# The hand-over from attention to the MLP, written out by hand up to step 8

## The chip, the core and the metric

The kernel runs on one core of a Trainium2 chip. The metric is the device time of a run in microseconds (us). The kernel before takes 806.33 us, the median of three runs from 805.54 to 807.37. The profiled execution is one more run of the same program. The engines are named as in the profile: PE (TensorE, matrix products), PEld (its weight loads), DVE (VectorE), ACT (ScalarE), POOL (GpSimd) and SP (SyncE, which issues DMAs). Each works off its own queue in order; semaphores tie the queues together.

## The reference

Two parts follow each other. The first is attention over 2 batches, 8 heads, 768 positions and 64 dimensions, in which a query sees only keys of its own cluster (the cluster is the centroid with the largest dot product of normalized vectors). The second is two MLP layers on the 1536 x 512 result.

```python
mask = q_assign[:, :, :, None] == k_assign[:, :, None, :]
scores = np.where(mask, scale * np.matmul(q, k.transpose(0, 1, 3, 2)), -1000000000.0)
attn = np.exp(scores - np.max(scores, axis=-1, keepdims=True))
attn = attn / (np.sum(attn, axis=-1, keepdims=True) + 1e-09)
x = np.matmul(attn, v)              # -> (1536 tokens, 512)
h = x @ w_in                        # layer 1: 512 -> 2048
g = np.maximum(h, 0.0) + alpha * np.minimum(h, 0.0)
x = g @ w_out                       # 2048 -> 512
h = x @ w_in2                       # layer 2
g = np.maximum(h, 0.0) + np.log1p(np.exp(-np.abs(h)))
out = g @ w_out2
```

## The kernel before

Every matrix product of the MLP is made of three, since an operand is held as a high and a low part (xh and xl for the tokens, ih/il and oh/ol for the two weights, gh and gl for the activated values): high by high, high by low, low by high.

**Attention.** The heads are taken as 8 pairs, and each pair as 12 units of 128 queries, so there are NU = 96 units. A loop over ticks u (L812) issues for each tick the scores of unit u (tile s, two banks), the exponentials of unit u-1 on ACT (L614), the transposes pt of unit u-2 (L627) with their copies ph on ACT (L643) and low parts pl on DVE (L647), and an output group o of an earlier unit (L657). A finished output is drained: copied by ACT (tmp, L680) and added by DVE (xs, L682). Steps of other work are hung on a tick by the table `todo`, at an early (E) or late (L) place in it. The end of each pair is `finish` (L698): sums plus epsilon on POOL, reciprocals on DVE, a broadcast rx on ACT (L729), three transposes rp on PE (L739), the division on DVE (L745), each in two halves, then xh on ACT (L752) and xl on POOL (L757). The table FINISH gives the ticks, FINISH_LAST those of the last pair.

**Weights.** They arrive as 64-bit words. `to_float32` (L152) converts one 128x512 tensor in seven turns: a DMA raw; m on ACT (L164); r on ACT and a clamp of m on DVE (L167, L168); a shift of m on DVE (L171); r on DVE (L173); t on POOL (L178); the high part on ACT (L180) and the low part on POOL (L181). A block F has two tensors, and there are 32 blocks; five are held at a time.

**MLP.** The 96 steps (layer, token group g of 512, block f) each have 24 products: 12 first products into hp (`first`, L876), and, after `activate` (ACT, L888 and L889) and `complete` (DVE L909, ACT gh L916, DVE gl L917), 12 second products into four accumulators acc (`second`, L935). After the last block of a group `close` moves the accumulators to y (L947, ACT). Blocks come in sets of 2, 4, 4, 4, 2 in layer 1, so steps 0 to 5 use two weight blocks for three token groups.

**What sets the order.** Up to tick 96 the written order of the code is each engine's order (`manual_schedule`). From there on (L813) a scheduler with its own model of time orders the rest, and may place it among the last manual ticks. The MLP's code starts after the attention pools are closed: `first` is called two steps ahead of `second`, and a step's conversions are written out all at once (`conversions`). The MLP's hp and acc lie in pools of PSUM of their own, opened after the attention.

Of the kernel before, what the change touches and what calls it, by code (L numbers as in the profile page):

```python
# [9 lines left out]
F32 = mybir.dt.float32  # L10
# [40 lines left out]
FINISH_LAST = [1, 2, 2, 3, 6, 7, 8, 9, 9]  # L51

BLOCKS = ((2, 4, 4, 4, 2), (4, 4, 4, 4))
P = 128
# [4 lines left out]
def kernel(  # L59
# [134 lines left out]

    with ExitStack() as actx:
# [5 lines left out]
        ps_s = actx.enter_context(tc.tile_pool(name="ps_s", bufs=2, space=PSUM))  # L201
        ps_t = actx.enter_context(tc.tile_pool(name="ps_t", bufs=2, space=PSUM))
        ps_o = actx.enter_context(tc.tile_pool(name="ps_o", bufs=1, space=PSUM))
        ps_m = actx.enter_context(tc.tile_pool(name="ps_m", bufs=1, space=PSUM))
# [3 lines left out]
        def warm(n):  # L208

            wps = ps_t.tile([P, 512], F32, tag="t", name="wps")  # L210
            for _ in range(n):
                nc.tensor.transpose(wps[:, 0:P], ident, ident)
# [56 lines left out]
        warm(18)  # L269
# [428 lines left out]
        def finish(n):  # L698
# [6 lines left out]
            ks = FINISH_LAST if last else FINISH  # L705
# [27 lines left out]
            for t in range(2):  # L733

                @at_(u0 + ks[4 + t])
                def _(t=t):
                    rp_ = ps_m.tile([P, 512], F32, tag="m", name="rp_")
                    for j in range(3):
                        nc.tensor.transpose(  # L739
                            rp_[:, j * P : (j + 1) * P],  # L740
                            q["rx"][:, 3 * t + j].rearrange("p h d -> p (h d)"),
                            ident,
                        )
                    xs = xs_[n]
                    nc.vector.tensor_tensor(out=xs[:, halves[t]], in0=xs[:, halves[t]], in1=rp_[:, 0:HS], op=ALU.mult)  # L745
# [8 lines left out]
            @at_(u0 + ks[8])  # L754
            def _():
                xs = xs_.pop(n)
                nc.gpsimd.tensor_tensor(  # L757
                    out=xl[:, i, where], in0=xs, in1=xh.bitcast(F32)[:, i, where], op=ALU.subtract
                )
# [26 lines left out]
        started = {}  # L786
        stage = {}
# [6 lines left out]
        def temp0(which, dtype):  # L794
            return stage["cpool"].tile([P, DM], dtype, tag=which, name=which, bufs={"raw": 3, "m": 2, "t": 2}.get(which, 1))
# [6 lines left out]
        for F in range(4):  # L802
            todo[NU - 14 if F < 2 else NU - 12 + 6 * F, L].append(lambda F=F: begin(F))
            for j in range(2):
                start = NU - 12 + 3 * (2 * F + j)
                for n, wait in enumerate((0, 2, 3, 4, 5, 6, 8) if F < 2 else (0,)):
                    tick = NU - 14 if n == 0 and 2 * F + j < 3 else start + wait
                    todo[tick, L].append(lambda F=F, j=j: next(started[F][j]))

        LAG = 2 + QT  # L810
        u = 0
        while u < NU + LAG + 2 or todo:  # L812
            if u == NU:  # L813
                man.close()
# [24 lines left out]
        man.close()  # L839
# [4 lines left out]
    gp = ctx.enter_context(tc.tile_pool(name="gp", bufs=2, reuse_waits="tile"))  # L844
    sp = ctx.enter_context(tc.tile_pool(name="sp", bufs=1, reuse_waits="tile"))
    cp = ctx.enter_context(tc.tile_pool(name="cp", bufs=2, side="right", reuse_waits="tile"))
    ps_h = ctx.enter_context(tc.tile_pool(name="ps_h", bufs=4, space=PSUM, reuse_waits="tile"))
    ps_a = ctx.enter_context(tc.tile_pool(name="ps_a", bufs=1, space=PSUM, reuse_waits="tile"))

    steps, starts, ends = [], set(), set()  # L850
    for layer in range(2):
        f0 = 0
        for size in BLOCKS[layer]:
            starts.add((layer, f0))
            ends.add((layer, f0 + size - 1))
            steps += [(layer, g, f) for g in range(NG) for f in range(f0, f0 + size)]
            f0 += size
    NS = len(steps)
    hps = {}
    mids = {}  # L860
    acts = {}
    accs = {}
    sums_ = {}

    def first(k):
        if k >= NS:
            return
        layer, g, f = steps[k]
        ts = slice(g * G, (g + 1) * G)
        h_, l_ = weights[layer, f][0:2]  # L870
        hp = ps_h.tile([P, G], F32, tag="h", name="hp")
        n = 0
        for c in range(NC_):
            cs = slice(c * P, (c + 1) * P)
            for a_, b_ in ((h_, xh), (h_, xl), (l_, xh)):
                nc.tensor.matmul(hp, lhsT=a_[:, cs], rhs=b_[:, c, ts], start=n == 0, stop=n == 3 * NC_ - 1)  # L876
                n += 1
        hps[k] = hp

    def activate(k):  # L880
        if k >= NS:
            return
        layer, g, f = steps[k]
        hp = hps[k]
        if layer == 0:

            n = gp.tile([P, G], F32, tag="n", name="n")
            nc.scalar.activation(out=n, in_=hp, func=AF.Relu, scale=-1.0)  # L888
            nc.scalar.activation(out=hp, in_=hp, func=AF.Relu)  # L889
            mids[k] = n  # L890
        else:

            a = gp.tile([P, G], F32, tag="n", name="a")
            nc.vector.tensor_scalar(  # L894
                out=a.bitcast(U32), in0=hp.bitcast(U32), scalar1=0x80000000, scalar2=None, op0=ALU.bitwise_or
            )
            sp_ = gp.tile([P, G], F32, tag="sp", name="sp")
            nc.scalar.activation(out=sp_, in_=a, func=AF.Softplus)  # L898
            mids[k] = sp_

    def complete(k):

        if k >= NS:
            return
        layer, g, f = steps[k]
        b_ = mids.pop(k)
        hp = hps.pop(k)
        if layer == 0:
            nc.vector.scalar_tensor_tensor(  # L909
                out=hp, in0=b_, scalar=nalpha[:, f : f + 1], in1=hp, op0=ALU.mult, op1=ALU.add  # L910
            )
        else:
            nc.vector.scalar_tensor_tensor(out=hp, in0=hp, scalar=0.0, in1=b_, op0=ALU.max, op1=ALU.add)
        gh = gp.tile([P, G], F32R, tag="gh", name="gh")
        gl = gp.tile([P, G], F32R, tag="gl", name="gl")
        nc.scalar.copy(out=gh, in_=hp)  # L916
        nc.vector.tensor_tensor(out=gl, in0=hp, in1=gh.bitcast(F32), op=ALU.subtract)  # L917
        acts[k] = gh, gl

    def second(k):  # L920
        layer, g, f = steps[k]
        gh, gl = acts.pop(k)
        h_, l_ = weights[layer, f][2:4]
        opens, closes = (layer, f) in starts, (layer, f) in ends
        if opens:
            for c in range(4):
                accs[c] = ps_a.tile([P, 512], F32, tag=f"acc{c}", name=f"acc{c}")
        for c in range(4):
            cs = slice(c * P, (c + 1) * P)
            if layer == 0:  # L930
                prods = ((h_[:, cs], gh), (h_[:, cs], gl), (l_[:, cs], gh))
            else:
                prods = ((gh[:, cs], h_), (gh[:, cs], l_), (gl[:, cs], h_))
            for n, (a_, b_) in enumerate(prods):
                nc.tensor.matmul(  # L935
# [137 lines left out]
```

## Time and profile before

| | |
|---|---|
| median of three runs | 806.33 us (805.54 to 807.37) |
| span of the profiled execution | 804.5 us, 1.83 us below that median |
| PE busy | 780.4 us (97%), 4139 products and transposes |
| PEld busy | 666.7 us (83%) |
| DVE busy | 585.3 us (73%) |
| ACT busy | 496.0 us (62%) |
| POOL busy | 356.8 us (44%) |
| chain that ended last | PE 78%, DVE 11%, ACT 3%, POOL 3%, issue 3% |

The profile is of one execution, for which the results give no device time beside the span. A busy share is an average over two stages: the attention, up to about 260 us, and the MLP after it. Products overlap on PE, so the time from one start to the next tells more than the duration in a row. The granted clock is given as a share of full speed: 1.00 is 2.4 GHz, 0.50 is 1.2 GHz, and values between are stretches with both.

### The profile page before, as it was taken

The numbers are of one execution on the slowest core, as the hardware profiler recorded it, in microseconds if no ns is written. First come the engines' busy times: TensorE is split into PE (matmuls) and PEld (weight loads), VectorE is DVE, ScalarE is ACT, GpSimd is POOL, SyncE is SP. The second block draws the span as 40 slices with busy tenths as digits, with TensorE's granted clock in tenths as the row PEclk, the third lists the DMA queues.
The fourth block names the chain that finished last, engine by engine and source line by source line (L and its number), as shares of the span: only waits on it lengthen the run. The fifth ranks groups of instructions, "written<-read, shape, count | busy, mean of one in ns | idle before, by whom it ended". The sixth has DMA issues, their size and how long they took to land.

```text
span 804.5 us, 11964 instructions
## 1 busy us (share of the span) xinstructions
PE 780.4 (97%) x4139; PEld 666.7 (83%) x4139; DVE 585.3 (73%) x923; ACT 496.0 (62%) x1024; POOL 356.8 (44%) x380
## 2 busy tenths in 40 slices
PE   6899999999998979999999999999999999999998
PEld 6789999999997758888888888888888888888886
DVE  7689989989989977547646835978469569765444
ACT  5788999999999778346536535674366245343221
POOL 6567668778354775026115404585144036023000
PEclk9899999999999989999999999999999999999999
DMA  9666667655552343102302401312014012000002
GB/s 265 180 166 172 152 170 173 182 145 128 119 144 64 105 157 132 53 26 79 105 0 72 138 1 53 132 53 78 1 53 156 2 53 81 24 2 1 28 31 97
DMA packets 26955, 75.91 MB, mean 94 GB/s; under 512 B 4464, under 2 KB 7408, under 8 KB 26896
## 3 DMA queue, kind: packets, MB, share of 16 engines
q1 hardware_dynamic: 26896, 75.16, 32.3%
q8 instruction: 32, 0.52, 0.3%
q14 instruction: 27, 0.22, 0.1%
HBM read 49.36 MB, written 3.15 MB: 65 GB/s over the span
## 4 chain that ended last, share of the span: by engine, by line
PE 78%; DVE 11%; ACT 3%; POOL 3%; issue 3%; DMA 1%; SPq 0%; DVEq 0%; POOLq 0%; ACTq 0%
PE acc L935 29%; PE hp L876 27%; PE pt L627 6%; PE o L657 6%; PE s L599 3%; PE s L600 3%; DVE r L173 2%; DVE pl L647 2%; POOL t L178 1%; DVE nm L605 1%; PE dps L403 1%; DVE m L168 1%; DVE y L950 1%; DVE lo L388 1%; ACT e L614 1%
## 5 line engine op out<-in xcount | busy, mean ns | idle before, releaser
L876 PE MATMUL hp<-xh,ih 128*128 128x512 f32 x384 | 150.2, 392 | 1.3 <-ACT e L614 1.3
L876 PE MATMUL hp<-xl,ih 128*128 128x512 f32 x384 | 150.1, 391 | 0.0
L876 PE MATMUL hp<-xh,il 128*128 128x512 f32 x384 | 149.9, 391 | 0.0
L181 POOL TENSOR_TENSOR il<-t,ih 128x512 fp32r<-128x512 f32 x32 | 44.3, 1385 | 198.7 <-ACT ih L180 188.3
L917 DVE TENSOR_TENSOR gl<-hp,gh 128x512 fp32r<-128x512 f32 x96 | 65.9, 686 | 69.6 <-ACT gh L916 69.5
L916 ACT CAST gh<-hp 128x512 fp32r<-128x512 f32 x96 | 56.4, 587 | 88.8 <-PE acc L935 69.9
L605 DVE TENSOR_REDUCE nm<-s 128x1 f32<-128x768 f32 x96 | 90.9, 947 | 18.3 <-PE s L600 18.3
L647 DVE TENSOR_TENSOR pl<-pt,ph 128x384 fp32r<-128x384 f32 x192 | 97.3, 548 | 5.8 <-ACT ph L643 4.9
L178 POOL TENSOR_TENSOR t<-m,r 128x512 uint32<-128x512 uint32 x64 | 85.6, 1337 | 30.8 <-DVE r L173 16.3
L643 ACT CAST ph<-pt 128x384 fp32r<-128x384 f32 x192 | 84.0, 485 | 14.7 <-PE pt L627 14.1
L614 ACT ACTIVATE e<-s,nm 128x768 f32<-128x768 f32 x96 | 87.9, 916 | 3.0 <-DVE nm L605 2.4
L898 ACT ACTIVATE sp<-a 128x512 f32<-128x512 f32 x48 | 30.4, 632 | 92.5 <-DVE a L894 92.5
L627 PE MATMUL pt<-ident,e 128*128 128x128 f32 x576 | 83.2, 277 | 4.1 <-DVE pl L647 4.0
L876 PEld LDWEIGHTS hp<-xh,ih 128*128 128x128 f32 x384 | 72.4, 189 | 16.5 <-ACT e L614 1.6
L876 PEld LDWEIGHTS hp<-xh,il 128*128 128x128 f32 x384 | 72.5, 189 | 15.2
L876 PEld LDWEIGHTS hp<-xl,ih 128*128 128x128 f32 x384 | 72.4, 189 | 15.1
L627 PEld LDWEIGHTS pt<-ident,e 128*128 128x128 f32 x576 | 66.9, 141 | 16.4 <-DVE pl L647 13.0
L935 PE MATMUL acc<-gh,oh 128*128 128x512 f32 x192 | 72.6, 395 | 5.4 <-ACT gh L916 5.4
L935 PE MATMUL acc<-gl,oh 128*128 128x512 f32 x192 | 75.7, 394 | 0.2 <-DVE gl L917 0.2
L935 PE MATMUL acc<-gh,ol 128*128 128x512 f32 x192 | 75.2, 392 | 0.0
L935 PE MATMUL acc<-ol,gh 128*128 128x512 f32 x192 | 74.7, 389 | 0.0
L935 PE MATMUL acc<-oh,gh 128*128 128x512 f32 x192 | 74.7, 389 | 0.0
(171 smaller groups left out, 1671.8 us busy)
## 6 DMA issues: line engine op xcount, KB each, us to landing
raw<-in_w_in_dram SPq DMA_DIRECT2D x32, 512.0 KB, 3.3
raw<-in_w_out_dram SPq DMA_DIRECT2D x32, 512.0 KB, 3.3
tok<-in_qk_tok_dram SPq DMA_DIRECT2D x8, 768.0 KB, 6.1
ak<-hi SPq DMA_DIRECT2D x31, 192.0 KB, 3.0
dim<-in_qk_dim_dram SPq DMA_DIRECT2D x6, 768.0 KB, 5.4
aq<-hi SPq DMA_DIRECT2D x16, 192.0 KB, 3.6
aq<-lo SPq DMA_DIRECT2D x16, 192.0 KB, 4.1
rawv<-in_v_dram SPq DMA_DIRECT2D x8, 384.0 KB, 3.5
```

Of the source, the lines that this page charges most:

```text
L178: nc.gpsimd.tensor_tensor(out=t.bitcast(U32), in0=mu, in1=r, op=ALU.add)
L181: nc.gpsimd.tensor_tensor(out=low, in0=t, in1=high.bitcast(F32), op=ALU.subtract)
L605: nc.vector.tensor_reduce(out=nm, in_=st[u]["s"][:, :, 0:HS], axis=AX.XY, op=ALU.max, negate=True)
L614: nc.scalar.activation(out=e.rearrange("p (a j) c -> p a (j c)", a=2), in_=st[u]["s"][:, :, 0:HS], func=AF.Exp, bias=st[u]["nm"], scale=1. ...
L627: nc.tensor.transpose(pt[:, j * P : (j + 1) * P], st[u]["e"][:, 3 * a + j, :], ident)
L643: nc.scalar.copy(out=dh, in_=src)
L647: nc.vector.tensor_tensor(out=dl, in0=src, in1=dh.bitcast(F32), op=ALU.subtract)
L657: nc.tensor.matmul(acc[key][:, 0:QG], lhsT=vv[:, j, 2 * hh : 2 * hh + 2, :].rearrange("p a d -> p (a d)"), rhs=grp[key][part][:, j, :], st ...
L876: nc.tensor.matmul(hp, lhsT=a_[:, cs], rhs=b_[:, c, ts], start=n == 0, stop=n == 3 * NC_ - 1)
L916: nc.scalar.copy(out=gh, in_=hp)
L917: nc.vector.tensor_tensor(out=gl, in0=hp, in1=gh.bitcast(F32), op=ALU.subtract)
L935: nc.tensor.matmul(accs[c], lhsT=a_, rhs=b_, start=opens and n == 0, stop=closes and n == 2)
```

## The change

The four PSUM pools of the attention are opened outside it, and the score pool (two tiles of two banks) is closed at tick 96. Its space is opened at once as ps_h, four single banks for hp. The accumulators no longer have a pool of their own; they take the two transpose banks, the output bank and the spare bank of the attention. The functions of the MLP are moved ahead of the attention's loop, unchanged but for these places and for `work`, which gives step 0 its tiles from the attention's buffers. A table hangs step 0 on ticks 96 to 101, its first products in two pieces, and the written order goes on to step 8 (MANUAL): first products three steps ahead, conversions in single turns (`pump`), begun three turns apart, four turns in a step. From step 8 the scheduler orders as before. Besides: the last pair but one finishes in ticks 87 to 98 (FINISH_NEXT), the last pair's two transpose groups come ahead of its two divisions, and its xl is made in two halves by DVE and POOL; the conversion of blocks 2 and 3 begins some ticks later; the tiles of the activation have four buffers where they had two.

```diff
-FINISH_LAST = [1, 2, 2, 3, 6, 7, 8, 9, 9]
+FINISH_NEXT = [3, 4, 5, 6, 7, 8, 9, 10, 14]
+FINISH_LAST = [1, 2, 2, 3, 3, 3, 5, 5, 5]
+MANUAL = 8
...
+    def first(k, chunks=(0, 1, 2, 3)):
+        if k not in hps:
+            hps[k] = stage["ps_h"].tile([P, G], F32, tag="h", name="hp")
+        for c in chunks:
...
+        if opens:
+            for c in range(4):
+                pool, tag = ((ps_t, "t"), (ps_t, "t"), (ps_o, "o"), (ps_m, "m"))[c]
+                accs[c] = pool.tile([P, 512], F32, tag=tag, name=f"acc{c}")
...
+    def enqueue(F):
+        for gen in started.pop(F, None) or convert(F, stage["wpool"], temp):
+            if F >= 4:
+                next(gen)
+            queue.append((max(turn[0], queue[-1][0] + 3 if queue else 0), gen))
+    def pump(n=1):
+        for _ in range(n):
+            for begun, gen in queue:
+                if begun <= turn[0] < begun + 6:
+                    next(gen)
+            turn[0] += 1
...
-            ks = FINISH_LAST if last else FINISH
+            ks = FINISH_LAST if last else FINISH_NEXT if n == len(pairs) - 2 else FINISH
...
+                if last:
+                    at_(u0 + ks[4 + t])(lambda t=t: spread(t))
+                    at_(u0 + 4)(lambda t=t: divide(t))
...
+                    for eng, cut in zip((nc.vector, nc.gpsimd), halves):
+                        eng.tensor_tensor(
+                            out=xl[:, i, where][:, cut], in0=xs[:, cut],
...
-        for F in range(4):
-            todo[NU - 14 if F < 2 else NU - 12 + 6 * F, L].append(lambda F=F: begin(F))
+        for F, tick in ((2, NU + 1), (3, NU + 4)):
+            todo[tick, L].append(lambda F=F: begin(F))
...
+        def banks_pass():
+            scores_ctx.close()
+            stage["ps_h"] = ctx.enter_context(tc.tile_pool(name="ps_h", bufs=4, space=PSUM, reuse_waits="tile"))
+        todo[NU, E].insert(0, banks_pass)
+        for tick, phase, fn in (
+            (0, L, lambda: first(0, (0, 1))),
+            (2, E, lambda: first(0, (2, 3))),
+            (2, E, lambda: activate(0)),
+            (2, L, lambda: enqueue(2)),
+            (2, L, pump),
+            (3, L, lambda: complete(0)),
+            (3, L, pump),
+            (4, L, lambda: first(2, (0, 1, 2))),
+            (4, L, pump),
+            (5, L, lambda: second(0)),
+            (5, L, lambda: first(1)),
+            (5, L, pump),
+            (5, L, lambda: first(2, (3,))),
...
-            if u == NU:
-                man.close()
...
-    gp = ctx.enter_context(tc.tile_pool(name="gp", bufs=2, reuse_waits="tile"))
+    stage["gp"] = ctx.enter_context(tc.tile_pool(name="gp", bufs=4, reuse_waits="tile"))
...
-    ps_a = ctx.enter_context(tc.tile_pool(name="ps_a", bufs=1, space=PSUM, reuse_waits="tile"))
...
+    activate(1)
+    activate(2)
+    for F in (3, 4):
+        enqueue(F)
+    complete(1)
+    pump()
+    first(3)
+    activate(3)
+    complete(2)
+    pump()
+    for k in range(1, MANUAL):
+        second(k)
+        close(k)
+        pump()
+        for F in due.get(k, []):
+            enqueue(F)
+        complete(k + 2)
+        pump()
+        first(k + 3)
+        activate(k + 3)
+        pump(2)
+    pump(20)
+    man.close()
+    for k in range(MANUAL, NS):
...
-    for k in range(NS):
-        complete(k + 1)
-        if k < 2:
-            conversions(k)
-        first(k + 2)
-        activate(k + 2)
-        second(k)
-        close(k)
-        if k >= 2:
-            conversions(k)
```

What this does to the queues is seen in the order of the instructions. PE, from the last-but-one group of transposes to the first output group behind step 0's products, before (rp are the transposes for a division, hp the first products, o the output):

```order
L739 MATMUL rp__4314<-ident,rx 128x128 x3
L627 MATMUL pt<-ident,e 128x128 x6
L876 MATMUL hp<-xh,ih 128x512
...
L876 MATMUL hp<-xh,il 128x512
L657 MATMUL o<-ph,vv 128x256 x6
L657 MATMUL o<-pl,vv 128x256 x6
L627 MATMUL pt<-ident,e 128x128 x6
```

The same place now, as far as the transposes for the last division:

```order
L760 MATMUL pt<-ident,e 128x128 x6
L790 MATMUL o<-ph,vv 128x256 x6
L231 MATMUL hp<-xh,ih 128x512
...
L231 MATMUL hp<-xh,il 128x512
L760 MATMUL pt<-ident,e 128x128 x6
L790 MATMUL o<-pl,vv 128x256 x6
...
L790 MATMUL o<-ph,vv 128x256 x6
L790 MATMUL o<-pl,vv 128x256 x6
L874 MATMUL rp__4346<-ident,rx 128x128 x3
L874 MATMUL rp__4350<-ident,rx 128x128 x3
```

An output group has moved ahead of step 0's products; these stand in two pieces with a transpose group and an output group between them, and the last division's transposes follow directly. ACT, the instructions ahead of the activated value gh of step 2, before (y copies an accumulator, oh and ih are high parts of weights, m and r steps of a conversion):

```order
L947 COPY y<-acc_4477 128x512
L947 COPY y<-acc_4478 128x512
L180 CAST oh<-t 128x512
L947 COPY y<-acc_4479 128x512
L164 ACTIVATE m<-raw 128x512
L167 ACTIVATE r<-raw 128x512
L947 COPY y<-acc_4480 128x512
...
L888 ACTIVATE n<-hp 128x512
L889 ACTIVATE hp<-hp 128x512
...
L916 CAST gh<-hp 128x512
```

ACT now, from the products of step 0 to the drain of the last output (rx is the broadcast for the division, tmp the copy of an output):

```order
L813 COPY tmp<-o 64x256
L250 ACTIVATE n<-hp 128x512
L251 ACTIVATE hp<-hp 128x512
L862 COPY rx<-rs 128x384
L182 CAST ih<-t 128x512
L166 ACTIVATE m<-raw 128x512
L862 COPY rx<-rs 128x384
L278 CAST gh<-hp 128x512
L169 ACTIVATE r<-raw 128x512
L813 COPY tmp<-o 64x256
L902 CAST xh<-xs 128x384 x2
```

Step 0's activation stands between two drains, with single turns of conversions among the broadcasts; the copies of accumulators, which stood ahead of n, come behind three activations.

## Rows read from the trace of the kernel before

**Rows 1.** stretches: length, busy us (instructions) by engine, clock, DMA share, GB/s

```profile
248.93:258.74 9.81, 7.75 (x52) 6.33 (x52) 9.57 (x16) 8.88 (x21) 4.40 (x6) 1.00 0.35 115
258.74:263.92 5.18, 3.56 (x27) 2.87 (x25) 5.14 (x10) 5.13 (x13) 1.93 (x2) 1.00 0.03 6
263.92:268.37 4.45, 4.45 (x12) 3.49 (x13) 4.36 (x8) 3.68 (x8) 4.29 (x4) 0.62 0.29 113
...
291.68:297.21 5.53, 0.15 (x1) 0.00 (x1) 5.46 (x9) 5.53 (x12) 3.56 (x3) 0.79 0.53 176
297.21:302.37 5.16, 5.12 (x13) 3.60 (x13) 5.12 (x8) 5.16 (x11) 3.28 (x3) 0.56 0.37 133
302.37:800.64 498.27, 498.11 (x2197) 411.90 (x2195) 320.69 (x472) 233.06 (x414) 159.60 (x119) 1.00 0.17 57
```

**Rows 2.** waits of PE, 240 to 320: us in total, times, longest

```profile
PE acc L935 <- ACT gh L916: 5.4, 1, 5.4
```

**Rows 3.** timeline of PE: start, us, line, output<-inputs, [idle before <-releaser]

```profile
258.74 0.34 PE L599 MATMUL s<-ak,aq 128*128 128x384 f32 x1
...
260.15 0.94 PE L657 MATMUL o<-pl,vv 128*128 128x256 f32 x6
261.38 0.55 PE L739 MATMUL rp__4314<-ident,rx 128*128 128x128 f32 x3 [0.28 <-ACT rx L729]
261.76 0.82 PE L627 MATMUL pt<-ident,e 128*128 128x128 f32 x6
263.92 0.61 PE L876 MATMUL hp<-xh,ih 128*128 128x512 f32 x1 [1.34 <-ACT e L614]
...
297.21 2.08 PE L935 MATMUL acc<-gh,oh 128*128 128x512 f32 x4 [5.38 <-ACT gh L916]
```

**Rows 4.** timeline of ACT, at the last scores and before the wait

```profile
260.81 0.51 ACT L729 COPY rx<-rs 128x384 f32<-128x384 f32 x1
...
262.49 0.36 ACT L680 COPY tmp<-o 64x256 f32<-64x256 f32 x1
262.88 0.90 ACT L614 ACTIVATE e<-s,nm 128x768 f32<-128x768 f32 x1
...
265.11 0.68 ACT L167 ACTIVATE r<-raw 128x512 uint32<-128x512 uint32 x1
...
292.93 0.61 ACT L888 ACTIVATE n<-hp 128x512 f32<-128x512 f32 x1
...
296.56 0.60 ACT L916 CAST gh<-hp 128x512 fp32r<-128x512 f32 x1
```

**Rows 5.** timeline of DVE at the hand-over

```profile
251.07 0.41 DVE L171 TENSOR_SCALAR m<-m 128x512 uint32<-128x512 uint32 x1
...
262.54 0.51 DVE L745 TENSOR_TENSOR xs<-xs,rp__4314 128x384 f32<-128x384 f32 x1
...
263.96 0.42 DVE L682 TENSOR_TENSOR xs<-tmp,o 64x256 f32<-64x256 f32 x1
...
269.38 1.39 DVE L171 TENSOR_SCALAR m<-m 128x512 uint32<-128x512 uint32 x1
```

**Rows 6.** groups of instructions by line: busy us in total, mean ns

```profile
L178 POOL TENSOR_TENSOR t<-m,r 128x512 uint32<-128x512 uint32 x64 | 85.6, 1337 | 30.8 <-DVE r L173 16.3 <-DVE m L171 10.4 <-PE acc L935 1.0
...
L917 DVE TENSOR_TENSOR gl<-hp,gh 128x512 fp32r<-128x512 f32 x96 | 65.9, 686 | 69.6 <-ACT gh L916 69.5
L173 DVE SCALAR_TENSOR_TENSOR r<-raw,r 128x512 uint32<-128x512 uint32 x64 | 61.8, 965 | 2.0 <-ACT r L167 1.0 <-issue 0.4
...
L171 DVE TENSOR_SCALAR m<-m 128x512 uint32<-128x512 uint32 x64 | 48.8, 762 | 1.1
...
L168 DVE TENSOR_SCALAR m<-m 128x512 f32<-128x512 f32 x64 | 45.0, 704 | 12.4 <-ACT m L164 12.2
L181 POOL TENSOR_TENSOR il<-t,ih 128x512 fp32r<-128x512 f32 x32 | 44.3, 1385 | 198.7 <-ACT ih L180 188.3 <-PE acc L935 10.4
...
L909 DVE SCALAR_TENSOR_TENSOR hp<-n,nalpha,hp 128x512 f32<-128x512 f32 x48 | 35.9, 749 | 34.1 <-ACT hp L889 34.1
```

More of the change, by code (lines that the diff above doesn't have):

```diff
@@ new lines @@
+    for layer in range(2):
+        f0 = 0
+        for size in BLOCKS[layer]:
+            starts.add((layer, f0))
+            ends.add((layer, f0 + size - 1))
+            mlp_steps += [(layer, g, f) for g in range(NG) for f in range(f0, f0 + size)]
+            f0 += size
+    NS = len(mlp_steps)
+    hps = {}
+    mids = {}
+    acts = {}
+    accs = {}
+    sums_ = {}
+    def first(k, chunks=(0, 1, 2, 3)):
+        if k >= NS:
+            return
+        layer, g, f = mlp_steps[k]
+        ts = slice(g * G, (g + 1) * G)
+        h_, l_ = weights[layer, f][0:2]
+        if k not in hps:
+            hps[k] = stage["ps_h"].tile([P, G], F32, tag="h", name="hp")
+        hp = hps[k]
+        for c in chunks:
+            cs = slice(c * P, (c + 1) * P)
+            for n, (a_, b_) in enumerate(((h_, xh), (h_, xl), (l_, xh))):
+                nc.tensor.matmul(
+                    hp, lhsT=a_[:, cs], rhs=b_[:, c, ts], start=c == 0 and n == 0, stop=c == NC_ - 1 and n == 2
+                )
@@ new lines, in second @@
+    def second(k):
+        layer, g, f = mlp_steps[k]
+        gh, gl = acts.pop(k)
+        h_, l_ = weights[layer, f][2:4]
+        opens, closes = (layer, f) in starts, (layer, f) in ends
+        if opens:
+            for c in range(4):
+                pool, tag = ((ps_t, "t"), (ps_t, "t"), (ps_o, "o"), (ps_m, "m"))[c]
+                accs[c] = pool.tile([P, 512], F32, tag=tag, name=f"acc{c}")
+        for c in range(4):
+            cs = slice(c * P, (c + 1) * P)
+            if layer == 0:
+                prods = ((h_[:, cs], gh), (h_[:, cs], gl), (l_[:, cs], gh))
+            else:
+                prods = ((gh[:, cs], h_), (gh[:, cs], l_), (gl[:, cs], h_))
+            for n, (a_, b_) in enumerate(prods):
+                nc.tensor.matmul(
+                    accs[c], lhsT=a_, rhs=b_, start=opens and n == 0, stop=closes and n == 2
+                )
@@ L850 @@
[L850 to L935, printed above, removed]
-                    accs[c], lhsT=a_, rhs=b_, start=opens and n == 0, stop=closes and n == 2
-                )
+    stage["cp"] = ctx.enter_context(tc.tile_pool(name="cp", bufs=2, side="right", reuse_waits="tile"))
@@ L939, in close @@
     def close(k):
-        layer, g, f = steps[k]
+        layer, g, f = mlp_steps[k]
         if (layer, f) not in ends:
```

140 lines of the change are left out of this document (102 added, 38 removed).

## The prediction, made before the result was known

> **What bounds the kernel now.** I read the kernel in stretches first, because a share over the whole span mixes two stages. The table of stretches [rows 1] shows TensorE (PE) without a gap from 302.37 us to the last product at 800.64: 498.11 us busy of 498.27, 2197 products, 0.2268 us each from start to start. That is the MLP, and nothing else bounds it there. All that can be won lies ahead of it, between the last attention scores at 258.74 and 302.37. In those 43.63 us PE has to do 108 of the 2304 MLP products (108 x 0.2268 = 24.5 us) and the rest of the attention: nine groups of 0.7 us (one of score products, three of six transposes, five of six output products; the starts 258.74 and 260.15 in [rows 3] hold two of them) and three short groups of transposes for the divisions (261.38 to 261.76, 0.38 each). That is 24.5 + 6.3 + 1.1 = 31.9, so some 11.7 us of the 43.63 are lost.
>
> The waits of PE [rows 2] then name the largest loss: 5.4 us, once, for the activated value gh. The timeline of PE [rows 3] puts it before 297.21, and the stretches show what follows: from 297.21 to 302.37 the granted clock is 0.56, and 12 products take 5.16 us, where 2.72 would do: 2.4 us. Earlier PE stands 1.34 us before its first MLP product at 263.92, and that product, too, meets a low clock: 263.92 to 268.37 at 0.62, 12 products in 4.45 us, 1.7 us too many. 5.4 + 2.4 + 1.3 + 1.7 = 10.8; the rest of the 11.7 are small gaps around the last transposes.
>
> The timeline of ScalarE (ACT) [rows 4] says why gh is late: its first step n starts at 292.93, gh follows at 296.56, and between them stand weight conversions; ACT is busy 5.53 of 5.53 us and VectorE (DVE) 5.46 [rows 1] while PE has 0.15. In the order of before nothing is left for PE to do at this point: products of the steps after it are behind the one that waits.
>
> **The change part by part.** PE's work is the same, 4139 matmuls in either order; the change moves it, so the sum is a comparison of when the same product count is reached. I take times in before's own span and write down when each engine reaches each place.
>
> First, the last pair but one finishes earlier. Its second broadcast on ACT, transposes and division on DVE are moved from after the last scores to ticks before them. DVE is full there, 9.57 of 9.81 us [rows 1], so the moved division (0.51 [rows 5]) pushes the last scores back: bounds 0 and 0.51, I take 0.5, as the engine has no hole to take it. Last scores: 259.2. It comes back on ACT: the last exponential, at 262.88, stands behind that broadcast (260.81, 0.51 us [rows 4]); without it, and with the shift, it starts where it was, near 262.9.
>
> Second, the hand-over. Single banks taken from the score buffers let the first products of step 0 be cut into two pieces of six, and an attention output group fills the time before. That group needs the drain on DVE which follows the copy at 262.49 [rows 4], so it starts at 263.4 and the first MLP product at 264.1, against 263.92 now. Six products 1.36, transposes 0.6, outputs 0.7, six products 1.36: 268.1. There are now 12 products done, as at 268.37 before, but a transpose group and an output group are done as well: 1.4 us ahead, and the low clock is not in it (a rival below).
>
> Third, the last drains. The next output group waits for a drain on DVE, and queued ahead of it are two weight conversions m, one on either side of the last subtractions pl. Such an m takes 0.41 or 1.39 us [rows 5]: short at 251.07, long at 269.38, where GpSimd (POOL) works beside it. The copy ahead of pl is itself held to 265.7, since ACT waits until POOL has read r (its next r starts at 265.11 [rows 4]). I reach 269.0 for the output group instead of 268.1: 0.9 lost, bounds 0 (both m short) and 1.4 (both long); I go towards the upper one, as POOL is busy 4.29 of the 4.45 us from 263.92 [rows 1]. The Trainium skill speaks against the change here ("SBUF — State Buffer", section "Who interferes with whom"): DVE in a two-port mode and GpSimd share a port pair, and the one that comes second is blocked for the other's whole instruction. The trace agrees in kind, 0.41 against 1.39. By that rule each m would wait out a full POOL instruction, and the sum would end 0.5 us higher.
>
> Outputs end at 270.4. The second transpose group of the last division waits for the sixth ACT instruction behind step 0's products (n, relu, broadcast, conversion, conversion, broadcast; 0.5 us each, as the broadcast's 0.51): 268.1 + 3.1 + 0.2 = 271.4, with 0.3 of transposes on either side 271.8. Lost 0.7, bounds 0 and 1.2. Nine products of step 2 (2.04): 273.8.
>
> Fourth, step 0's second products open their accumulators in the attention's own banks. The second bank comes free with the last division on DVE, and that is late: a low part on POOL (1.385 [rows 6]) after the conversion at 270.3, then t (1.337 [rows 6]), only then ACT's next r, then the copy of the output (0.36 at 262.49 [rows 4]), the drain (0.42 [rows 5]) and two divisions (0.51 [rows 5]). That is 270.3 + 1.4 + 1.3 + 0.6 + 0.4 + 0.4 + 1.0 = 275.4, while PE is there at 274.5 with its first three products done. Lost 0.9, bounds 0 and 1.8 (POOL's instructions one place later). Nine products: 277.5.
>
> Fifth, the steps to 8 in written order. From 277.5 on 12 + 3 + 12 + 12 = 39 products follow, 8.85 us: 286.3. What hides step 1's activation: when its products end, 3 + 12 products or 3.4 us stand before the second products that want it, and n, relu, combination, gh, gl take about 3.4; I cost this at nothing, with 0.2 lost if the cover is short. From there the first products run three steps ahead, so 24 products or 5.44 us lie between the products of a step and their use; the 5.4 us wait has a cover as long as itself. Conversions begin 3 turns apart, and 4 turns make a step: 4/3 of a weight tensor in each step. DVE's part is then 4/3 x (0.704 + 0.762 + 0.965) + 0.749 + 0.686 = 4.7 us of 5.44 [rows 6], so they fit. DMA and SP: the same 64 weight loads, and the four that are asked for later are wanted only from step 6 on.
>
> At 286.3 there are 12 x 6 = 72 products done. The 108th ends 36 x 0.2268 = 8.2 us later, at 294.5, where before has 302.37. After step 8 the order is again the scheduler's, with the same two steps' lead as in the gapless stretch [rows 1], and costs nothing new. The sum is 302.37 - 294.5 = 7.8 us. The span of 804.5 becomes 796.7. The median of the runs lies 1.83 us above that span, within their scatter (805.54 to 807.37); with the same distance the forecast is 798.5 us. If every bound of the waits is zero the gain is 10.8 (795.5), if all are at their upper end 5.9 (800.4).
>
> **The rivals.** One, the clock falls at the hand-over all the same. For it: in 258.74 to 263.92 PE was busy 3.56 of 5.18 us and the granted clock then fell [rows 1]; the new order still has gaps there. Against: it has an output group more in them, and 248.93 to 258.74 was busy 7.75 of 9.81 at 1.00. Price: the 1.7 us that 263.92 to 268.37 lost, 800.2 us. The Trainium skill ("TensorE: Matmul & The Clock Gate", section "What's actually happening") says that the watch on PE runs free of the kernel; by that some runs would show the drop and others not.
>
> Two, slower: DVE can't carry conversions and activations of steps 1 to 7 in a fixed order. For it: m at 1.39 instead of 0.41, and DVE and ACT both full from 291.68 to 302.37 [rows 1]. With two long m and a long r (1.4 each) in each tensor, a step needs 4/3 x 4.2 + 1.44 = 7.0 us and not 5.44; seven steps then lose 1.6 x 7 = 11 us, which ends at 809.5. It decides from (5.44 + 7.8/7 =) 6.55 us for a step. Against: POOL has 4/3 x 2.72 = 3.6 us of work in a step, so not every instruction can meet it.
>
> Three, the written order is followed but the gain is lost again: the conversions are taken at a slower pace than in before, and the scheduler behind step 8 finds weights not ready, so that a wait of 5 to 7 us returns there. For it: in before the same wait arose two steps after the scheduler took over. Against: by the order of the changed kernel the weights of blocks 0 to 6 are converted by then, and the two-step lead is the same. Price: about all of the gain, 804 to 806 us.
>
> Four, all late banks are covered: 795.5 us, if POOL's part on the chain at the fourth step is shorter than I count.
>
> **How the numbers follow.** The forecast 0.62, the clock 0.15, DVE too slow 0.06, lost again 0.06, all covered 0.11. The range goes from 795.8, which leaves out only the far end of the covered case, to 801.8, which takes in the clock (800.2), the upper bounds (800.4) and part of both together (802.1). A measurement of this kernel can tell 0.2%, 1.6 us. Faster by more: 0.62 + 0.15 + 0.11 and a bit of the lost-again case, 0.89; within: 0.05; slower: 0.06.
>
> **What would show it.** Right: the first MLP product near 264 at a clock of 1.00; PE waits for the drain (about 0.9), the broadcast (0.7) and the division at the second accumulator (0.9), and no wait over 1.5 us up to step 8; the 5.4 us wait for gh gone; the gapless stretch of 2196 products begins some 8 us earlier and still takes 498 us. Wrong: a low clock after 264 or 270; PE waiting for gh or gl in steps 1 to 7; a gap after step 8.

## The result and the profile after

The changed kernel takes 800.13 us, the median of four runs (799.23 to 800.71), against 806.49 (805.54 to 807.37) for the kernel before beside it: a ratio of 0.991, with a 95% interval of 0.9893 to 0.9928. The forecast was 798.5 us, and the range 795.8 to 801.8 holds the time. The gain is 6.4 us where the sum had 7.8.

The profiled execution has a span of 798.9 us. Its stretches, with the columns of [rows 1]. The first ends, as there, at the last scores, the second at the first MLP product; the third holds step 0's first products, the fourth goes on to the place that 302.37 us is in before, and the fifth is the gapless rest:

```profile
249.62:259.42 9.80, 8.41 (x60) 6.94 (x58) 9.56 (x17) 8.94 (x22) 4.26 (x5) 1.00 0.35 115
259.42:264.68 5.26, 4.19 (x31) 3.35 (x29) 4.17 (x8) 5.21 (x13) 2.17 (x2) 1.00 0.11 19
264.68:269.20 4.52, 4.33 (x26) 3.39 (x24) 3.37 (x8) 2.50 (x7) 3.49 (x4) 1.00 0.24 96
269.20:295.65 26.45, 24.58 (x115) 20.03 (x115) 16.41 (x27) 18.69 (x37) 11.83 (x9) 1.00 0.33 120
295.65:795.06 499.41, 498.67 (x2197) 411.69 (x2195) 332.94 (x484) 242.96 (x428) 170.10 (x127) 1.00 0.18 60
```

From the last scores (259.42) to the place of 302.37 us in before (295.65, the 109th MLP product, with 2196 to go; the counts of 2197 include one that runs across the border) it takes 36.23 us, where before took 43.63 [rows 1]: 7.4 us won. The clock is 1.00 throughout. The last stretch has the same products and takes 499.41 us, where it took 498.27: 1.1 us are given back there.

The waits of PE from 240 to 330 us, which answer to [rows 2]: the 5.4 us wait for gh is gone, and the longest that has come is 1.01 us.

```profile
PE o L790 <- DVE xs L815: 1.5, 3, 0.7
PE pt L760 <- DVE pl L780: 1.2, 3, 0.5
PE acc L298 <- DVE xs L883: 1.0, 1, 1.0
PE rp__4350 L874 <- ACT rx L862: 0.9, 1, 0.9
PE hp L231 <- POOL il L183: 0.3, 1, 0.3
```

The timeline of PE, with the marks that the prediction set times for (first a score product of tick 88, seven ticks before the last, then the last score product, the drains, step 0, the last broadcast, the second accumulator, the 73rd MLP product, two waits further on, and the last product):

```profile
240.39 0.42 PE L732 MATMUL s<-ak,aq 128*128 128x384 f32 x1
...
259.95 0.34 PE L733 MATMUL s<-mk,mq 80*128 80x384 f32 x1
...
263.86 0.98 PE L790 MATMUL o<-ph,vv 128*128 128x256 f32 x6 [0.66 <-DVE xs L815]
264.68 0.40 PE L231 MATMUL hp<-xh,ih 128*128 128x512 f32 x1
...
269.20 0.97 PE L790 MATMUL o<-ph,vv 128*128 128x256 f32 x6 [0.20 <-DVE xs L815]
...
272.08 0.55 PE L874 MATMUL rp__4350<-ident,rx 128*128 128x128 f32 x3 [0.86 <-ACT rx L862]
...
276.37 0.50 PE L298 MATMUL acc<-gh,oh 128*128 128x512 f32 x1 [1.01 <-DVE xs L883]
...
287.49 0.39 PE L231 MATMUL hp<-xh,ih 128*128 128x512 f32 x1
...
315.56 0.50 PE L231 MATMUL hp<-xh,il 128*128 128x512 f32 x1 [0.26 <-POOL il L183]
...
537.31 0.50 PE L298 MATMUL acc<-gl,oh 128*128 128x512 f32 x1 [0.46 <-DVE gl L279]
...
794.83 0.39 PE L298 MATMUL acc<-oh,gl 128*128 128x512 f32 x1
```

What PE waits for at the hand-over, from the timelines of the engines that it waits for: the conversions m, the second broadcast, the copy tmp of the last output behind the conversion r, the last division, and the last pair's low part in its two halves.

```profile
265.71 0.42 DVE L170 TENSOR_SCALAR m<-m 128x512 f32<-128x512 f32 x1
...
268.06 0.63 DVE L173 TENSOR_SCALAR m<-m 128x512 uint32<-128x512 uint32 x1
...
275.77 0.55 DVE L883 TENSOR_TENSOR xs<-xs,rp__4350 128x384 f32<-128x384 f32 x1
...
276.57 0.55 DVE L909 TENSOR_TENSOR xl<-xs,xh 128x384 fp32r<-128x384 f32 x1
...
271.53 0.49 ACT L862 COPY rx<-rs 128x384 f32<-128x384 f32 x1
...
273.75 0.67 ACT L169 ACTIVATE r<-raw 128x512 uint32<-128x512 uint32 x1 [1.24 <-POOL t L180]
274.45 0.36 ACT L813 COPY tmp<-o 64x256 f32<-64x256 f32 x1
...
276.94 1.05 POOL L909 TENSOR_TENSOR xl<-xs,xh 128x384 fp32r<-128x384 f32 x1 [3.22 <-ACT xh L902]
```

### The profile page after: what moved, and what is told of

The parts are those of the page before. It is cut to its first block, busy times and chain, and to the rows that moved or that the text cites. A ratio compares the mean times of both kernels' runs of the same rounds, so it can differ in the third digit from the quotient of the medians.

```text
span 798.9 us, 11860 instructions
## 1 busy us (share of the span) xinstructions
PE 778.7 (97%) x4139; PEld 664.4 (83%) x4139; DVE 583.9 (73%) x924; ACT 497.4 (62%) x1024; POOL 354.8 (44%) x380
## 5 line engine op out<-in xcount | busy, mean ns | idle before, releaser
L180 POOL TENSOR_TENSOR t<-m,r 128x512 uint32<-128x512 uint32 x64 | 84.6, 1322 | 27.9 <-DVE r L175 18.1
L298 PE MATMUL acc<-gh,oh 128*128 128x512 f32 x192 | 74.3, 390 | 1.0 <-DVE xs L883 1.0
```

The source lines that it names most:

```text
L180: nc.gpsimd.tensor_tensor(out=t.bitcast(U32), in0=mu, in1=r, op=ALU.add)
L298: nc.tensor.matmul(accs[c], lhsT=a_, rhs=b_, start=opens and n == 0, stop=closes and n == 2)
```

## What the trace of before had to say, read again

The prediction explained the wait for gh by the weight conversions that stand between n and gh on ACT; call this theory A. It did not ask why n is so late. The profile of before answers that with rows that the prediction did not use (one of POOL, two of PE, two of ACT):

```profile
284.18 2.03 POOL L757 TENSOR_TENSOR xl<-xs,xh 128x768 fp32r<-128x768 f32 x1
...
288.50 0.62 PE L876 MATMUL hp<-xl,ih 128*128 128x512 f32 x2
288.95 0.39 PE L876 MATMUL hp<-xh,il 128*128 128x512 f32 x1
...
289.20 0.62 ACT L180 CAST oh<-t 128x512 fp32r<-128x512 f32 x1 [1.69 <-POOL t L178]
...
292.37 0.69 ACT L167 ACTIVATE r<-raw 128x512 uint32<-128x512 uint32 x1
```

The last pair's low part xl ends at 286.2 us, 26.9 us behind the last score product (259.27). On POOL it stands behind conversions. The last first products of steps 2, 3 and 4 need it, and the scheduler has set them together, behind step 1's second products: step 2's last two are the second product of the row at 288.50 and the one at 288.95, the 84th and 85th of the MLP. PE does not wait for xl there: the order is late, not the operand. The product at 288.95 ends at 289.3, but n of step 2 starts only at 292.93 [rows 4], because ACT, in its order, first works off conversions and two copies y. So PE does everything that can be done first, then the lump, and then nothing is left while gh of step 2 is made. In after, the first half of xl ends at 277.1, 17.2 us behind the last score product, and step 2's last first product is the 48th. Theory B is that the late xl is the cause: steps 2 and 3 (tokens 512 to 1023) need only the first half of the last pair's 768 tokens (768 to 1151), and get it late.

## The experiments

All times are medians of fresh runs, and the ratios are to the kernel before on the same chip (807.24, 807.08 and 806.52 us in the three sets). Since the attention's length varies between executions (see the last section), I compare traces by the time from the start of the last score product to the end of the last product: 541.5 us in before (259.27 to 800.80), 535.3 in after (259.95 to 795.22). Each is one execution, and 1.7 us of the 541.5 are a low clock at the first MLP product that other executions with the same wait there don't show (see the rivals). The place of a product in PE's order is counted in the instructions of each kernel.

**Scheduler from step 1.**

```diff
-MANUAL = 8
+MANUAL = 1
...
-    pump(20)
     man.close()
+    pump(30)
```

> The kernel after, but the scheduler takes over behind step 0 and not at step 8: the last ticks of the attention, the early divisions, the low part in halves and step 0 stay as they are. Theory A (the 5.4 us wait of before comes from weight conversions that stand in lumps ahead of the activations on ACT and DVE, and the written order of steps 1 to 7 with single turns removes it): a wait for gh or gl of 3 to 6 us comes back between 280 and 300 us, 804 to 806 us. Theory B (the wait comes from the last pair's low part xl, which POOL delivers late, so that the first products of several steps end together; the changed last ticks of the attention remove it): no wait over 1.5 us, 799.5 to 801.5 us.

802.87 us (800.29 to 804.12), ratio 0.9935 (0.9911 to 0.9959); 536.7 us from the last score product. The time lies between the two forecasts, 1.4 us above B's and 1.1 us below A's. No wait for gh came back. Behind step 0 there are only waits for gl, over the whole MLP:

```profile
PE acc L298 <- DVE gl L279: 1.9, 3, 0.8
```

Theory A's 3 to 6 us did not come. By the traces the written order of steps 1 to 7 is worth 1.4 us of the 6.3, by the ratios about 2.0 (0.9935 against 0.991, whose intervals overlap); the rest is won ahead of it.

**Attention's end in written order, MLP by the scheduler.**

```diff
-            if u == NU:
-                man.close()
```

> The kernel before, but the written order is kept up to the attention's last tick, and only the MLP is left to the scheduler. The last divisions then keep their written places and xl is still whole, on POOL. Theory A: the lumps of conversions are as before, the wait for gh stays at 4 to 6 us, 805 to 807 us. Theory B: it depends on when xl comes; if it comes 2 us or more earlier than at 286 us, the wait shrinks by as much, 802 to 804 us; if not, 805 to 807 us. Theory C (written order at the hand-over alone is what gains): 800 to 801.5 us.

809.18 us (807.51 to 811.46), ratio 1.0024 (1.001 to 1.0037); 544.0 us: slower than before, and 2.2 us above the highest forecast. PE stands 4.5 us for gh and 3.7 for drains. xl on POOL is no earlier than in before: it ends 27.9 us behind the last score product.

```profile
284.06 1.86 POOL L757 TENSOR_TENSOR xl<-xs,xh 128x768 fp32r<-128x768 f32 x1 [1.37 <-ACT xh L752]
...
298.61 0.80 PE L933 MATMUL acc<-gh,oh 128*128 128x512 f32 x1 [4.54 <-ACT gh L914]
```

Written order of the attention's end by itself gains nothing (theory C falls). A and B both allow the wait; the longer time neither forecast.

**The kernel before with the low part in halves, DVE and POOL.**

```diff
+                if last:
+                    for eng, cut in zip((nc.vector, nc.gpsimd), halves):
+                        eng.tensor_tensor(
+                            out=xl[:, i, where][:, cut], in0=xs[:, cut],
+                            in1=xh.bitcast(F32)[:, i, where][:, cut], op=ALU.subtract,
+                        )
+                    return
```

> The kernel before with one part of the change alone: the last pair's xl is made in two halves by DVE and POOL. The same weight conversions stand on ACT and DVE. Theory A: the wait for gh stays at 4 to 6 us and the low clock behind it, 805 to 807 us. Theory B: the first products of the steps end one after the other, the wait falls under 1.5 us and the clock behind it is 1.00, 799 to 801.5 us.

801.36 us (800.31 to 802.52), ratio 0.9922 (0.9902 to 0.9943); 536.9 us. One part of the change alone, with all conversions in place, moves the time nearly as far as the whole change. The first half ends 17.2 us behind the last score product, on DVE:

```profile
274.21 1.64 DVE L759 TENSOR_TENSOR xl<-xs,xh 128x384 fp32r<-128x384 f32 x1
...
283.72 1.20 POOL L759 TENSOR_TENSOR xl<-xs,xh 128x384 fp32r<-128x384 f32 x1
...
303.54 0.50 PE L883 MATMUL hp<-xh,ih 128*128 128x512 f32 x1 [2.67 <-DVE gl L924]
```

In the order that the scheduler makes now, step 2's last first product is the 38th of the MLP, where it was the 85th. Theory A falls as the whole cause. B has the time, but not the row: it wanted no wait over 1.5 us and a clock of 1.00, and a few steps later a first product waits 2.67 us for gl, with 0.62 behind it (last section).

**The same halves, both on POOL.** One word differs from the diff above: `(nc.gpsimd, nc.gpsimd)`.

> The kernel before with the last pair's xl in two halves, both on POOL. The first half then stands five places earlier in POOL's queue than the whole xl did; DVE gets nothing new, and the conversions stay. Theory B (group 1 of the tokens, steps 2 and 3, needs the first half alone): the first half ends some 8 us earlier than xl in before, the wait for gh falls under 3 us, 799.5 to 803 us. Rival (it was the help of DVE that counted): the wait stays at 4 to 6 us, 805 to 808 us.

801.89 us (800.72 to 803.61), ratio 0.994 (0.9924 to 0.9956); 535.5 us, near the 535.3 of after. The fresh runs gain 4.6 us, and of the 6.0 between the traces 1.7 are the low clock of before, which the halves don't touch. The longest wait is 1.3 us, the one at the first MLP product that before had too. POOL's timeline has the first half five places earlier than the whole:

```profile
277.97 1.18 POOL L759 TENSOR_TENSOR xl<-xs,xh 128x384 fp32r<-128x384 f32 x1 [0.67 <-ACT xh L752]
...
288.87 1.19 POOL L759 TENSOR_TENSOR xl<-xs,xh 128x384 fp32r<-128x384 f32 x1
```

The second half ends at 290.1, as late as the whole did in before (27.5 us behind the last score product), and costs nothing. So it is the half that steps 2 and 3 need, and not DVE's help. Here, too, step 2's last first product is the 38th.

**Conversions of blocks 2 to 4 left out on ACT and DVE.**

```diff
+        if plain:
+            nc.gpsimd.tensor_copy(out=high, in_=w0)
+            nc.gpsimd.tensor_copy(out=low, in_=w0)
+            yield
+            return
```

> The kernel before, with the conversions of blocks 2 to 4 left out on ACT and DVE (36 instructions): POOL makes both parts of these weights by plain copies, two for each tensor as before, so that the values are not those of the reference. xl still stands behind some ten such instructions on POOL, and the last first products of three steps still wait for it. Theory A: without conversions on ACT and DVE the wait for gh falls under 1 us, 798 to 801 us. Theory B: xl is as late as before, PE stands 4 to 6 us in all for xl or gh between 280 and 300 us, 804 to 807 us.

799.35 us (798.0 to 800.27), ratio 0.9894 (0.9876 to 0.9913); 533.6 us. The wait for gh is 1.39 us:

```profile
278.89 1.85 POOL L762 TENSOR_TENSOR xl<-xs,xh 128x768 fp32r<-128x768 f32 x1
...
293.53 0.73 PE L940 MATMUL acc<-gh,oh 128*128 128x512 f32 x2 [1.39 <-ACT gh L921]
```

Theory A has the time (798 to 801 forecast) and nearly the wait (under 1 us); B's 804 to 807 us did not come. It doesn't separate them as meant, since without the conversions xl itself ended 19.6 us behind the last score product instead of 26.9. But its order on PE kept the lump: step 2's last first product is the 90th. n follows it at once; in before n comes 3.6 us behind it, with conversions in front:

```profile
290.39 0.39 PE L881 MATMUL hp<-xh,il 128*128 128x512 f32 x1
...
290.87 0.60 ACT L893 ACTIVATE n<-hp 128x512 f32<-128x512 f32 x1 [1.63 <-PE hp L881]
```

From n to the second product it takes 2.7 us here and 4.3 in before (292.93 to 297.21 [rows 3, 4]). So, once step 2's products are late in the order, most of the wait is what stands on ACT in front of the activation: theory A is one half of the cause, and the late products are the other. What the conversions cost with xl itself as late as in before was not obtained and stays open.

**The last pair but one finished early, in the kernel before.**

```diff
-            ks = FINISH_LAST if last else FINISH
+            ks = FINISH_LAST if last else FINISH_NEXT if n == len(pairs) - 2 else FINISH
```

> The kernel before with another part of the change alone: the last pair but one finishes in ticks 87 to 98 (FINISH_NEXT), everything else as before, the last pair's xl whole on POOL behind the same conversions. Theory B (what counts is when the first products of steps 2 and 3 can get the last pair's xl): xl stays at 26 to 27 us behind the last score product, the wait for gh stays at 4 to 6 us, 805 to 808 us. Rival (the crowded last ticks are the cause): the wait shrinks under 2 us, 800 to 803 us. For the prediction's first step: the moved division costs the last scores 0.5 us, or nothing, against the same order's start at tick 88.

806.69 us (804.69 to 808.19), ratio 0.9996 (0.9982 to 1.0009); 541.1 us. xl ends 25.2 us behind the last score product, and the wait is there, longer than before:

```profile
283.03 2.04 POOL L758 TENSOR_TENSOR xl<-xs,xh 128x768 fp32r<-128x768 f32 x1
...
296.97 2.07 PE L936 MATMUL acc<-gh,oh 128*128 128x512 f32 x4 [6.16 <-ACT gh L917]
```

As B expects, if a little longer than its 4 to 6 us; the rival falls. n of step 2 starts 5.5 us behind that step's last first product (287.19 to 292.69), with conversions and four copies y ahead of it on ACT. From the score product at tick 88 to the last scores it takes 18.94 us (240.36 to 259.30), 19.06 in before: the moved division pushes nothing back.

**The kernel after with the low part whole.** The seven lines of the halves are taken out again.

> The kernel after, with the last pair's xl whole on POOL again as in before; PE's order stays the same. Theory (what the low part in halves is worth depends on the order of PE's products, not on the second by which xl comes): xl ends 1 us later, near 279 us, and the first product that needs it starts near 280 us, so no new wait and 800.1 us as for after, within 0.3%. Rival (a late xl costs by itself): PE waits 1 to 2 us for POOL at the last products of step 1, 801 to 802 us.

799.63 us (799.22 to 802.11), ratio 0.9918 (0.9893 to 0.9942); 535.2 us, no new wait. xl ends 19.0 us behind the last score product, since the last divisions of the changed order are early. So there are two ways to the same gain: to make the needed half early, whereupon the scheduler moves step 2's products up, or the hand-over in its written order with early divisions, which sets them at the 48th place by hand. The halves add nothing to the second. No run has the changed order with a late xl, so whether that order alone would do is not shown.

Over the nine traces of before, after and the kernels so far, the part of xl that steps 2 and 3 wait for ends 25.2 to 27.9 us behind the last score product in three (541.1 to 544.0 us to the end) and 16.6 to 19.6 in six (533.6 to 536.9). No trace lies between. PE waits for xl in none of them: in the three late ones the order has step 2's last first product at the 68th to 85th place with the conversions ahead of n, and the kernel without conversions is fast with the 90th.

**Both broadcasts ahead of step 0's activation, in the kernel after.**

```diff
-FINISH_LAST = [1, 2, 2, 3, 3, 3, 5, 5, 5]
+FINISH_LAST = [0.5, 0.7, 1.5, 1.5, 3, 3, 5, 5, 5]
```

> The kernel after, with the reciprocals and both broadcasts rx of the last pair put ahead of step 0's activation on DVE and ACT. Theory (each of the four waits at the hand-over stands on PE's path by itself): the wait of 0.86 us for the second rx is gone, the 1.01 us for the second accumulator shrinks by at most 0.3, nothing new; 534.4 us from the last score product to the end of the last product, against 535.3. Rival (the wait moves on): the second accumulator's wait grows to 1.9 us, 535.3 us.

One run, 799.0 us, so no interval; 534.9 us. The wait for rx is gone, but the one for the second accumulator has grown from 1.0 to 1.6 us:

```profile
PE acc L298 <- DVE xs L883: 1.6, 1, 1.6
```

The rival is nearer: of the 0.86 us only 0.35 are gained. The waits are in a row, and the last one sets the end.

**The same, and one turn of the conversions a tick later.**

```diff
+FINISH_LAST = [0.5, 0.7, 1.5, 1.5, 3, 3, 5, 5, 5]
...
-            (3, L, pump),
...
-            (4, L, pump),
+            (4, L, lambda: pump(2)),
```

> The kernel after, with both broadcasts ahead of step 0's activation, and one turn of the conversions moved a tick later, so that on ACT the copy of the last output stands ahead of the long conversion r. Theory: the waits of 0.86 us (rx) and 1.01 us (second accumulator) are both gone, 1.5 to 1.9 us in all, 798.2 to 798.6 us where after has 800.1, and 533.4 to 533.8 us from the last score product to the end. Rival (DVE and POOL are then the next to be late): at most 0.5 us gained.

797.59 us (796.73 to 798.15), ratio 0.9882 (0.9864 to 0.9901); 533.0 us. Both waits are gone, and the trace is 2.3 us shorter than that of after, more than the 1.5 to 1.9 forecast. It is faster than before, and by the trace and the ratios (0.9882 against 0.991, whose intervals just meet) also than after.

**The same, with written order to step 16.** `MANUAL = 16`.

> The same, with the written order going on to step 16. Theory (the small waits behind step 8, 0.3 to 0.5 us each, come from the lumps that the scheduler makes when it takes over): those before 330 us go, another 0.5 to 0.8 us less than with the two moves alone. Rival (the scheduler's start is only put off): the same waits come behind step 16, no difference beyond 0.2 us.

803.56 us (801.88 to 804.45), ratio 0.9956 (0.9939 to 0.9973); 537.8 us. Both expectations fail: it is 6 us slower than with the scheduler from step 8, 4.8 by the traces. The small wait for il ahead of 330 us (0.25 us) stays, since it falls on step 9's first products, which stand in written order in both kernels. The stretches 310 to 350 and 350 to 400 us, here (first two rows) with PE's longest wait, and then for the kernel that hands over at step 8:

```profile
310.00:350.00 40.00, 39.75 (x176) 32.60 (x175) 20.90 (x30) 16.21 (x30) 9.18 (x7) 1.00 0.12 40
350.00:400.00 50.00, 46.33 (x202) 37.33 (x201) 42.28 (x56) 32.17 (x59) 24.27 (x18) 1.00 0.34 114
...
398.69 0.50 PE L298 MATMUL acc<-gl,oh 128*128 128x512 f32 x1 [2.22 <-DVE gl L279]
```

```profile
310.00:350.00 40.00, 39.75 (x175) 32.61 (x175) 29.66 (x45) 23.84 (x44) 15.61 (x12) 1.00 0.31 102
350.00:400.00 50.00, 50.00 (x222) 41.40 (x222) 36.13 (x52) 26.68 (x48) 17.95 (x14) 1.00 0.24 81
```

In the written order DVE does 20.90 us in the first 40 where it does 29.66 under the scheduler; the work comes behind step 16, DVE goes to 42.28 of 50, and PE waits for gl and gh. The written rule begins a block's conversion only when its buffer's last user has been issued; that the scheduler begins its earlier turns sooner is my reading of the code and was not tried by itself. This is the prediction's third rival, at a later place.

**Both moves, scheduler from step 1.** `MANUAL = 1` on top of the two moves.

> The kernel with both moves at the hand-over (broadcasts first, one turn of the conversions later), and the scheduler takes over behind step 0 instead of step 8. Theory (the written order of steps 1 to 7 is worth 1.4 us, as between the kernel after and its variant with the scheduler from step 1): 534.4 us from the last score product to the end of the last product, 798.5 to 800 us. Rival (the scheduler's small waits and those of the hand-over are the same slack, and only one of the two has to go): 533.0 to 533.5 us, 797.5 to 798 us.

800.4 us (799.25 to 800.87), ratio 0.9918 (0.9903 to 0.9932); 534.8 us, 1.8 more than with written order to step 8. The waits for gl add up to 2.4 us. The time is 0.4 us above the theory's range, but 534.8 is near its 534.4 and not the rival's 533.0 to 533.5. By the trace the theory holds: the written steps 1 to 7 and the waits of the hand-over are separate.

## Why the prediction was right, and where it was not

The time was right and so were the places, but the step on which most of the gain rests was explained by half.

**The step that failed** is the account of the 5.4 us: that the activation is late because conversions stand in front of it on ACT, and that steps to 8 in written order, with a three-step lead as cover, take the wait away. Conversions do stand in front: 3.6 us pass on ACT between step 2's last first product and n, and without the conversions the wait is 1.39 us. But they cost this only because the scheduler has put step 2's products at the 85th place, and that goes with xl of the last pair. The low part in halves on POOL, with all conversions in place, takes the 5.4 us wait and the low clock behind it away, and the scheduler from step 1 keeps all but 1.4 us of the gain. So the written steps to 8 are not what removes the wait. Their cover was miscounted, too: by the order of the changed kernel 48 products, not 24, lie between step 4's first and second products, and before has 63 there. The sum did not need the cause, because it only counted products to a common place with no wait in it; so it came out near, for a reason it did not have; that part was luck. The prediction named the low part on POOL in its fourth step only as something that delays other work.

**First step.** The push-back of 0.5 us did not happen. The last scores are 0.68 us later than in before (259.42 against 258.74 [rows 3]), but the score product at tick 88 was so already (240.39 against 239.68). The lower bound, 0, was right: the moved work fitted beside what DVE had.

**Second step.** First MLP product 5.26 us behind the last scores (4.9 forecast), at a clock of 1.00; step 0's products are done at about 268.8.

**Third step.** 0.9 us for the drain were forecast and 0.20 measured: the conversions took 0.42 and 0.63 us, near the short end of [rows 5]. I chose the upper end since POOL was busy, but a share of a stretch doesn't say what POOL does beside one instruction: the first m met none of its conversion work, the second, at 268.06, only the last 0.35 us of its xl (266.56 for 1.85). The rule weighed there (the Trainium skill, "SBUF — State Buffer", section "Who interferes with whom") lets the second to come wait for the first; the rows agree in kind, with 0.21 us on top of 0.42 where 0.35 us of the first were left. The broadcast: 0.7 forecast, 0.86 measured.

**Fourth step.** 0.9 forecast and 1.01 measured, by the chain forecast: r held by t, tmp behind r, then the divisions.

**Fifth step.** No wait between 276.4 and 295.6 us, as forecast. The 109th product starts at 295.65 (294.5 forecast), of which 0.7 us is the later start. Net of that the hand-over gained 7.4 us, as the table of stretches says; up to 1.7 of it is the low clock in this one trace of before (the rivals, below).

**Behind the 109th product** nothing was to be lost, and 1.1 us were: a wait of 0.26 us at step 9's first products, still in written order, one of 0.46 us under the scheduler, and 0.6 us more busy time (498.67 against 498.11); before has one of 0.2 us there. The 7.4 less these 1.1 is 6.3; the medians have 6.4.

**The rivals.** The clock did not fall in after, but the reason need not be the new order. In the kernel with the halves on POOL the same instructions, with the same 1.3 us before the first MLP product, ran at 1.00, where before had 0.62 [rows 1], and so they did with the halves on both engines and without conversions:

```profile
267.21:271.50 4.29, 4.29 (x24) 3.77 (x25) 4.20 (x8) 4.19 (x10) 4.13 (x4) 1.00 0.29 110
```

So up to 1.7 us of the difference between the traces of before and after is chance in the one execution of before, and the sum counted them as won. This fits the Trainium skill ("TensorE: Matmul & The Clock Gate", section "What's actually happening"): the watch runs free of the kernel, and by that one order can meet a fall or not. How often before meets it, its one trace does not say. The third rival (the gain lost again behind step 8) did not come in after: 1.1 us were lost there, not 5 to 7. No run took up the second, DVE too slow, by itself; the table of waits has none for gh or gl in the written steps.

## What to carry to other kernels

Where an engine waits for an activation, look at the instructions in front of it, and then past them for what made its first products late; here the two together made the wait, and one subtraction far down another engine's queue had put the products late in the scheduler's order. If only part of a tensor is needed first, produce that part as an instruction of its own: it was worth 4.6 and 5.9 us, where the rewritten hand-over gave 6.4. When waits stand in a row, take out the last one too, or the gain stays with it.

## What was not expected of the hardware

The same attention code takes different times. The last score product starts between 257.99 and 262.59 us in the traces; the granted clock from 15 to 240 us was 0.99 in the earliest and 0.97 in the latest, so comparisons of traces by absolute time can be off by as much as 4.6 us, more than most steps here.

Idle PE and the clock behind it: after waits of 5.38, 6.16 and 4.54 us the clock was 0.56 [rows 1], 0.52 and 0.51; after 2.67 us (halves on DVE and POOL) it was 0.62; after 2.22 us (written order to step 16) it stayed 1.00. These are the stretches from the end of the last two waits:

```profile
303.54:307.98 4.44, 4.44 (x12) 3.52 (x13) 4.41 (x8) 4.13 (x9) 2.21 (x3) 0.62 0.61 202
```

```profile
398.69:403.50 4.81, 4.81 (x21) 4.00 (x22) 4.81 (x9) 1.87 (x4) 0.00 (x0) 1.00 0.66 217
```

The same subtraction for half of xl took 1.64 us on DVE where it started 0.17 us behind a conversion t on POOL (274.04, 1.39 us, in the kernel before with the halves on both engines), and 0.55 us in after, where POOL was idle when it started.
